# Eight memory recalls as three f32r products each, in an attention and gated-FFN kernel on one Trainium2 core

## The chip, the cores and the metric

The kernel runs on one core of one Trainium2 chip. The metric is the device time of one execution in microseconds (us), lower is better. A time is the median of several runs of the compiled program. Beside it one execution is taken by the hardware profiler; its span reaches from the first to the last instruction of the core.

Five engines work on their own instruction queues: TensorE (PE in the profile, with its weight loads as PEld), VectorE (DVE), ScalarE (ACT), GpSimd (POOL) and SyncE (SP), which issues most DMAs here.

## What is computed

The input x is 2048 tokens of 448 values. After a layer norm it goes through 16-head attention with a compressive memory (four segments of 512 tokens, attended one by one) and, in parallel, through a gated FFN of width 1792. Both results are added to x.

```
xn = layernorm(x)                              # [2048, 448]
q, k, v = xn @ wq, xn @ wk, xn @ wv            # 16 heads of 28, 4 segments of 512 tokens
for each segment s:
    a_dot = softmax(q_s k_s^T * scale + mask) v_s
    a_mem = (phi(q_s) M) / (phi(q_s) z + 1e-6) # phi(t) = t + 1 if t > 0 else exp(t)
    o_s   = g * a_mem + (1 - g) * a_dot        # g = sigmoid(beta), one per head
    M, z  = M + phi(k_s)^T v_s, z + sum(phi(k_s))
out = x + o @ wo + (sigmoid(xn w_gate) * (xn w_up)) @ w_down
```

The step `phi(q_s) M` is called a recall below. The first segment has an empty memory, so there are three segments with recalls, and in each the sixteen heads are done in four groups of four heads: twelve recalls in all.

## The kernel before, in words

The program has a front part (up to about 163 us), in which the projections, the memory and the recalls are made block by block (a block is a segment of 512 tokens, `b` = 0 to 3), and then a long part in which the FFN's matmuls and the attention scores are interleaved by a fixed ratio, and at the end the output projection.

**Precision.** TensorE takes operands of type f32 or f32r. [...] Where a result must be good to f32, the kernel splits each operand into a high part (the value rounded by an ACT copy to f32r) and a low part (the value less its high part, a DVE subtraction) and adds up three f32r products: high by high, low by high, high by low. The projections `pv` and `pp`, the FFN and the output projection all work so; with 448 inputs in four chunks that makes the eleven products of the list `TERMS`. The recalls of before are the exception: each is one matmul of two f32 operands.

**A block of the front part.** The order on PE, ACT and DVE is the order in which the code is written (`manual_schedule`). For block `b`:

1. Four values steps, `t` = 0 to 3: `values(b, t)` makes eleven products into the PSUM tile `pv` (L335), and ACT copies it into `vst` (L339). In blocks 2 and 3 a recall of the block before, `recall(b-1, t-1, ...)`, follows from `t` = 1 on; the fourth one comes after the first chunk of keys and queries.
2. Seven chunks of keys and queries, `k` = 0 to 6: `keys_queries` makes eleven products into `pp` (L355); ACT writes the high part to `qk` (L356) and makes exp of the negative part in `e` (L360, L361); DVE writes the low part (L362) and finishes the feature map phi in `e` (L365). SP stores `qk` in `qd` (L363) and the query features in `fd` (L368).
3. From chunk `k` = 2 on, `key_rows` transposes the key features of chunk `k` - 2 on PE (`pk`, L375; `e` is the operand loaded as weights) and ACT copies them to `kn` (L377). From `k` = 4 on, `update` makes the memory's increment on PE (`pmm`, L383) and DVE adds it (L389, L390).
4. Meanwhile the layer norm of block `b` + 1 is made: `statistics` on DVE (L294 to L296), `root` on ACT with a load of the square root's table (L301), `rstd` and `normalise` on DVE (L308 to L320), and `turn`, which transposes the normalised tokens on PE (`pt`, L95) and splits them into `xs` on ACT (L97) and DVE (L102, L103).

**A recall.** `phi_queries` loads the query features of a head group from `fd` (L394, SP). PE multiplies them by the group's memory `mst` into the PSUM tile `n2` (L401), which alternates between the banks `m` and `pd`. `pk` and `pmm` use the same two banks. DVE transposes the result (L402), divides and weighs it (L132 to L136) and transposes it back (L404); POOL's queue stores it in `od` (L405). In blocks 2 and 3 the recalls concern the blocks 1 and 2; the recalls of block 3 itself come at the end of the front part, between FFN matmuls.

```
        def recall(b, i, phi):
            ...
            n2 = bank("n2", ("m", "pd")[i % 2])
            T.matmul(n2, mst[b % 2][i], phi, start=True, stop=True)
            V.transpose(ts, n2)
            weigh(sb, ts, gate[:, i:i + 1], MEM_EPS)
            V.transpose(tb, ts)
```

`four_k` is a pool of four buffers of 4 KB per partition: in the front part its tenants are the `qk` tiles.

Of the kernel before, what the change touches and what calls it, by code (L numbers as in the profile page):

```python
# [9 lines left out]
F32 = mybir.dt.float32  # L10
F32R = mybir.dt.float32r
AF = mybir.ActivationFunctionType
# [4 lines left out]
P = 128  # L17
# [6 lines left out]
NT = 4  # L24
# [3 lines left out]
NG = H // HG  # L28
GW = HG * DH
# [32 lines left out]
def kernel(  # L62
# [11 lines left out]
    V, A, G, T = nc.vector, nc.scalar, nc.gpsimd, nc.tensor  # L74
# [33 lines left out]
    def x_block(b):  # L108
        return x[b * L:(b + 1) * L, :].rearrange("(t p) d -> p t d", p=P)
# [5 lines left out]
    def bank(name, tag):  # L115
        return ps.tile([P, L], F32, name=name, tag=tag, bufs=banks[tag])
# [10 lines left out]
    def weigh(pool, num, g, add):  # L127

        r = pool.tile([P, 16], F32, name="rc", bufs=2)
        n3 = num.rearrange("p (m c) -> p m c", c=32)  # L130
        if add:
            V.tensor_scalar_add(r, n3[:, :, DH], add)  # L132
            V.reciprocal(r, r)
        else:
            V.reciprocal(r, n3[:, :, DH])
        V.scalar_tensor_tensor(n3[:, :, :DH], n3[:, :, :DH], g, r.unsqueeze(2).to_broadcast([P, 16, DH]),  # L136
                               op0=ALU.mult, op1=ALU.mult)
# [11 lines left out]
    def four_k(dtype, name):  # L149
        return mid.tile([P, 2, L], dtype, name=name, tag="4k", bufs=4)  # L150
# [125 lines left out]
    with tc.tile_pool(name="front", bufs=2) as sb, tc.manual_schedule(engines=FRONT):  # L276
# [4 lines left out]
        wv = [late_pair("wv") for _ in range(4)]  # L281
        wv = [wv[c // 2][:, c % 2, :] for c in range(8)]
        wqk = [sb.tile([P, 8, P], F32R, name=f"wqk{c}", bufs=1) for c in range(7)]
        mst = [[sb.tile([GW, P], F32, name=f"mst{n}_{i}", bufs=1) for i in range(NG)] for n in range(2)]
        one = sb.tile([P, 1], F32, name="one", bufs=1)
        kn = eight_k(F32, "kn").rearrange("p (t a) n -> p t (a n)", t=NT)

        def statistics(b, t0, steps):

            stats = sb.tile([P, steps, 6], F32, name=f"stats{steps}")  # L290
            mv = sb.tile([P, steps, 2], F32, name=f"mv{steps}")
            vh = sb.tile([P, steps], F32, name=f"vh{steps}")
            for t in range(steps):
                V.bn_stats(stats[:, t, :], acc[b][:, t0 + t, :])  # L294
                V.bn_aggr(mv[:, t, :], stats[:, t, :])
            V.tensor_scalar(vh, mv[:, :, 1], EPS, -0.5, op0=ALU.add, op1=ALU.mult)  # L296
            return mv, vh
# [94 lines left out]
        def phi_queries(b, i):  # L392
            phi = sb.tile([GW, L], F32, name="phi", tag="e", bufs=5)
            nc.sync.dma_start(phi, fd[b][i * GW:(i + 1) * GW])  # L394
            return phi

        def recall(b, i, phi):
            ts = sb.tile([P, L], F32, name="ts", bufs=1)
            tb = sb.tile([P, L], F32, name="tb", bufs=2)
            n2 = bank("n2", ("m", "pd")[i % 2])  # L400
            T.matmul(n2, mst[b % 2][i], phi, start=True, stop=True)  # L401
            V.transpose(ts, n2)  # L402
            weigh(sb, ts, gate[:, i:i + 1], MEM_EPS)
            V.transpose(tb, ts)  # L404
            nc.gpsimd.dma_start(od[b][P * i:P * (i + 1)], tb)  # L405
# [98 lines left out]
        for b in range(NB):  # L504
            last = b == NB - 1
            phi, xn = {}, {}
            if b > 1:
                phi = {i: phi_queries(b - 1, i) for i in range(NG)}
            st = None
            for t in range(3 if b == 0 else 0, NT):  # L510
                values(b, t)
                if b > 1 and t > 0:
                    recall(b - 1, t - 1, phi[t - 1])
                if b == 0:
                    split_qk(t)
                if last:
                    continue
                if t == (3 if b == 0 else 0):
                    mv, vh = statistics(b + 1, 0, NT)
                if t == (3 if b == 0 else 0):  # L520
                    st = mv, vh, root(vh)
                if t == (3 if b == 0 else 2):
                    A.activation(one, ident[:, 0:1], AF.Exp)
            if st and b > 0:
                st = rstd(*st)
                for n in range(2):
                    xn[n] = normalise(b + 1, n, *st[n])
            e = {}
            for k, c in enumerate((3, 4, 5, 6, 0, 1, 2) if last else range(7)):
                e[c] = keys_queries(b, c)  # L530
                if b == 0 and c + 4 < 7:
                    split_qk(c + 4)
                if k == 0:
                    if b > 1:
                        recall(b - 1, NG - 1, phi[NG - 1])
                    if b == 0:
                        st = rstd(*st)
                    if b == 0:
                        A.activation(gate, gate, AF.Exp, scale=-1.0)
                        V.tensor_scalar_add(gate, gate, 1.0)  # L540
                        V.reciprocal(gate, gate)
                        V.tensor_scalar(gate_n, gate, -1.0, 1.0, op0=ALU.mult, op1=ALU.add)
                if (b, k) in ((0, 3), (1, 0)):
                    with tc.issue_after(stored[b, c]):
                        nc.sync.dma_start(acc[b + 2], x_block(b + 2))
                if (b, k) in ((2, 1), (3, 0)):
                    with tc.issue_after(stored[b, c]):
                        next(ffn)
                if last:
                    if k > 0:  # L550
                        next(ffn)
                    if 2 <= k < 6:
                        phi[k - 2] = phi_queries(b, k - 2)
                    if k > 4:
                        begin[k - 5]()
                        recall(b, k - 5, phi[k - 5])
                    continue
                if 2 <= k < 6:
                    key_rows(k - 2, e[k - 2])
                if 4 <= k:  # L560
                    update(b, k - 4)
                if k == 6:
                    update(b, 3)
                n = k - 1 if b == 0 else k + 1
                if 2 <= n < 6:
                    turn(b + 1, n - 2, xn[n - 2])
                if 0 <= n < 4 and n not in xn:
                    xn[n] = normalise(b + 1, n, *st[n])
                if b == 2 and k == 6:
                    next(ffn)  # L570
            if last:
                for i in range(2):
                    for _ in range(FILLS[i]):
                        next(ffn)
                    if i == 0:
                        begin[2]()
                    recall(b, i + 2, phi[i + 2])
# [3 lines left out]
    sb = ctx.enter_context(tc.tile_pool(name="att", bufs=1, reuse_waits="tile"))  # L581
# [203 lines left out]
    with tc.manual_schedule(engines=MANUAL):  # L785
        next(steps)
        k = sum(FILLS) + 6
# [46 lines left out]
```

## Time and profile before

| | |
|---|---|
| median of 3 runs | 687.41 us (687.2 to 687.65) |
| the profiled execution, its own time | 687.43 us |
| its span | 685.7 us |
| PE busy | 679.6 us of the span |
| DVE / ACT / POOL busy | 566.7 / 341.6 / 147.6 us |
| the recall matmuls (L401), busy | 12.3 us, 24 records for 12 recalls |
| block 2 of the front part on PE | 77.88 to 114.82 us |
| block 3 of the front part on PE, up to the first attention scores | 114.82 to 163.18 us |

How to read it: a row of the timeline gives the start and the length of a merged run of equal instructions, the engine, the line of the kernel, the tiles (out<-in) and the count. Matmuls are pipelined, so lengths overlap; what one run of matmuls costs PE is the distance from its start to the start of the next run. Square brackets tell how long the engine sat idle before and who ended it. `SPq` rows are DMA issues on SyncE's queue.

### The profile page before, as it was taken

What the parts mean: (1) busy time and instruction counts of PE and PEld (TensorE: products, weight loads), DVE (VectorE), ACT (ScalarE), POOL (GpSimd) and SP (SyncE); (2) the same over time, 40 slices, a digit from 0 to 9 for tenths busy, and PEclk for the clock granted to TensorE, in tenths of its full rate; (3) what the DMA queues carried; (4) which work ended last, traced back from release to release, by engine and by line L of the source; (5) the groups of instructions that cost most, each with busy time, mean ns of one, the idle gap of its engine ahead of it and who ended that gap; (6) DMA issues with size and microseconds to landing.
All of it is one profiled execution on the core that took longest, in us unless ns stands there. A gap on an engine that the chain in (4) does not pass through costs nothing.

```text
span 685.7 us, 10450 instructions
## 1 busy us (share of the span) xinstructions
PE 679.6 (99%) x3594; PEld 565.5 (82%) x3594; DVE 566.7 (83%) x994; ACT 341.6 (50%) x563; POOL 147.6 (22%) x349
## 2 busy tenths in 40 slices
PE   8999999999999999999999999999999999999997
PEld 7898878778878787887878778787887878778897
DVE  6765695767789998988998889988998899889863
ACT  4837555343554455544556446455643465446220
POOL 3500010101223232222232222232321323212000
PEclk9999999999999999999999999999999999999999
DMA  7446556697242333243324243324342423423342
GB/s 268 179 153 233 204 207 244 246 337 179 71 95 78 94 87 86 58 127 83 85 58 112 58 127 70 99 57 117 82 102 69 97 56 86 95 78 91 93 155 107
DMA packets 45796, 84.37 MB, mean 123 GB/s; under 512 B 6320, under 2 KB 20400, under 8 KB 45232
## 3 DMA queue, kind: packets, MB, share of 16 engines
q1 hardware_dynamic: 42736, 76.37, 36.4%
q0 software_dynamic: 3008, 7.34, 5.2%
q8 instruction: 28, 0.46, 0.3%
q14 instruction: 24, 0.20, 0.1%
HBM read 51.05 MB, written 32.64 MB: 122 GB/s over the span
## 4 chain that ended last, share of the span: by engine, by line
PE 97%; DMA 1%; DVE 1%; SPq 0%; issue 0%; ACT 0%; ACTq 0%
PE pgu L247 41%; PE pd L173 20%; PE pp L355 10%; PE st L612 6%; PE pa L687 5%; PE po L771 5%; PE pv L335 5%; PE pmm L383 2%; PE n L401 2%; DMA acc<-in_x 1%; PE pt L95 1%; PE pk L375 1%; DMA vv<-vd 0%; DVE stats L294 0%; DVE acc L775 0%
## 5 line engine op out<-in xcount | busy, mean ns | idle before, releaser
L247 PE MATMUL pgu<-xs,wgu 128*128 128x512 f32 x1232 | 303.6, 393 | 0.0
L247 PEld LDWEIGHTS pgu<-xs,wgu 128*128 128x128 f32 x1232 | 228.2, 188 | 46.9 <-issue 2.4
L173 PE MATMUL pd<-wdn,hh 128*128 128x448 f32 x672 | 155.9, 367 | 0.0
L173 PEld LDWEIGHTS pd<-wdn,hh 128*128 128x128 f32 x672 | 122.4, 188 | 12.0 <-issue 0.8
L627 POOL TENSOR_SCALAR_AFFINE_SELECT w<-w 128x256 f32<-128x256 f32 (+1 forms) x160 | 80.3, 505 | 240.9 <-ACT w L616 192.4
L667 ACT ACTIVATE w<-w 128x1024 f32<-128x1024 f32 (+1 forms) x96 | 87.4, 916 | 88.4 <-DVE w L666 87.9
L666 DVE TENSOR_TENSOR w<-w,mb 128x1024 f32<-128x1024 f32 (+1 forms) x96 | 98.6, 1035 | 0.2
L616 ACT ACTIVATE w<-st 128x512 f32<-128x512 f32 x128 | 74.7, 591 | 43.2 <-PE st L612 42.9
L629 DVE TRANSPOSE_TENSOR_REDUCE mx<-w 128x32 f32<-128x1024 f32 x64 | 78.8, 1231 | 14.8 <-POOL w L627 14.7
L355 PE MATMUL pp<-xs,wqk 128*128 128x512 f32 x308 | 77.7, 401 | 0.0
L174 DVE TENSOR_TENSOR acc<-pd,acc 128x448 f32<-128x448 f32 x112 | 67.2, 600 | 1.1 <-PE pd L173 1.1
L355 PEld LDWEIGHTS pp<-xs,wqk 128*128 128x128 f32 x308 | 56.8, 188 | 13.4 <-issue 2.4
L612 PE MATMUL st<-qk 84*128 84x128 f32 (+3 forms) x256 | 62.3, 313 | 0.1
L258 ACT ACTIVATE hh<-sg 128x512 fp32r<-128x512 f32 x56 | 35.2, 628 | 53.4 <-DVE sg L256 42.2
L612 PEld LDWEIGHTS st<-qk 84*128 84x128 f32 x256 | 47.7, 189 | 7.5 <-ACT w L616 0.7
L255 ACT ACTIVATE sg<-pgu 128x512 f32<-128x512 f32 x56 | 33.1, 592 | 36.2 <-PE pgu L247 36.2
L656 DVE STREAM_TRANSPOSE mb<-top 128x1024 f32<-128x1024 f32 x32 | 39.7, 1242 | 12.6 <-POOL top L653 12.3
L362 DVE TENSOR_TENSOR qk<-pp,qk 128x512 fp32r<-128x512 f32 x28 | 19.3, 689 | 29.8 <-ACT e L360 23.7
L259 DVE SCALAR_TENSOR_TENSOR hh<-sg,hh 128x512 fp32r<-128x512 f32 x56 | 38.9, 694 | 2.8 <-ACT hh L258 2.4
L335 PE MATMUL pv<-wv,xs 128*128 128x448 f32 x176 | 39.6, 376 | 0.4 <-DVE xs L102 0.3
L256 DVE SCALAR_TENSOR_TENSOR sg<-sg,pgu 128x512 f32<-128x512 f32 x56 | 37.3, 667 | 1.7 <-PE pgu L247 1.5
L687 PE MATMUL pa<-w,vv 128*32 128x128 f32 (+3 forms) x512 | 37.9, 436 | 0.0
(100 smaller groups left out, 639.5 us busy)
## 6 DMA issues: line engine op xcount, KB each, us to landing
qk<-qd SPq DMA_DIRECT2D x192, 112.0 KB
qd<-qk SPq DMA_DIRECT2D x28, 512.0 KB
raw<-in_w_ffn SPq DMA_DIRECT2D x14, 512.0 KB
vd<-vst SPq DMA_DIRECT2D x4, 1024.0 KB
vv<-vd SPq DMA_DIRECT2D x16, 256.0 KB
od<-w POOLq DMA_DIRECT2D x16, 256.0 KB, 3.9
sums<-od SPq DMA_DIRECT2D x32, 128.0 KB
out<-acc SPq DMA_DIRECT2D x16, 224.0 KB
```

The lines of the kernel that those rows point to most:

```text
L173: T.matmul(pd[:, :D], l, r, start=n == 0, stop=n == len(mms) - 1)
L174: V.tensor_add(acc[b][:, t, :], pd[:, :D], acc[b][:, t, :])
L247: T.matmul(dst, wgu[f][:, w, side * P:(side + 1) * P], xs[b][:, a, :], start=n == 0, stop=n == len(TERMS) - 1)
L335: T.matmul(pv[:, :D], xs[b][:, a, t * P:(t + 1) * P], wv[w], start=n == 0, stop=n == len(TERMS) - 1)
L355: T.matmul(pp, wqk[c][:, w, :], xs[b][:, a, :], start=n == 0, stop=n == len(TERMS) - 1)
L612: T.matmul(st[:, at:at + L - kb * P], self.qk[:KS, 1, h, kb * P:(kb + 1) * P], self.qk[:KS, 0, h, kb * P:], start=True, stop=True)
L616: A.activation(w, st, AF.Copy)
L627: G.affine_select(d, d, pattern=pattern, base=0, channel_multiplier=-1, compare_op=ALU.is_ge, fill=MASK)
L629: V.tensor_reduce(mx[:, 16 * (n - 1):16 * (n + 1)], w3[:, n // 2, :2 * L].rearrange("p (b n) -> p b n", n=32), axis=mybir.AxisListType.X, ...
L666: V.tensor_sub(w, w, m)
L667: A.activation(w, w, AF.Exp, scale=SCALE)
L687: T.matmul(pa[32 * j:32 * j + 32, kb * P:], self.vv[:, kb, 32 * j:32 * j + 32], self.pairs[j // 2].block(j % 2, kb), start=kb == 0, stop=k ...
```

## The change

The eight recalls of blocks 1 and 2 (those made during blocks 2 and 3) become three f32r products each. The four recalls of block 3 stay f32 matmuls.

- `memory_parts` splits the memory of all four head groups at once, at the start of a block: an ACT copy and a DVE subtraction of 112x512, into the tile `ms`. For that the four memory tiles of a parity become one tile.
- `parts` splits the features of one head group, 112x512 again, into `phis`. Group 0 is split at the start of the block, group `t` + 1 after `values(b, t)`, so a group is split two values steps before its recall.
- `ms` and the four `phis` tiles take buffers of the pool `four_k`.
- `statistics` now stands ahead of the recall of its step (it was behind it; in step 0 there is none). `root` comes one step later in block 2 (`t` = 1), and `turn` one chunk later there (chunks 2 to 5, they were 1 to 4), with the normalisation of tokens 2 and 3.

```diff
--- before.py
+++ after.py
@@ -281,7 +281,8 @@
         wv = [late_pair("wv") for _ in range(4)]
         wv = [wv[c // 2][:, c % 2, :] for c in range(8)]
         wqk = [sb.tile([P, 8, P], F32R, name=f"wqk{c}", bufs=1) for c in range(7)]
-        mst = [[sb.tile([GW, P], F32, name=f"mst{n}_{i}", bufs=1) for i in range(NG)] for n in range(2)]
+        memory = [sb.tile([GW, NG, P], F32, name=f"mst{n}", bufs=1) for n in range(2)]
+        mst = [[m[:, i, :] for i in range(NG)] for m in memory]
         one = sb.tile([P, 1], F32, name="one", bufs=1)
         kn = eight_k(F32, "kn").rearrange("p (t a) n -> p t (a n)", t=NT)
 
@@ -394,11 +395,27 @@
             nc.sync.dma_start(phi, fd[b][i * GW:(i + 1) * GW])
             return phi
 
+        def memory_parts(b):
+
+            m = four_k(F32R, "ms")[:GW].rearrange("p a (i n) -> p a i n", i=NG)
+            A.activation(m[:, 0], memory[b % 2], AF.Copy)
+            V.tensor_sub(m[:, 1], memory[b % 2], m[:, 0].bitcast(F32))
+            return m
+
+        def parts(i, phi, m):
+
+            f = four_k(F32R, "phis")[:GW]
+            A.activation(f[:, 0, :], phi, AF.Copy)
+            V.tensor_sub(f[:, 1, :], phi, f[:, 0, :].bitcast(F32))
+            return [(m[:, a, i, :], f[:, w, :]) for a, w in ((0, 0), (1, 0), (0, 1))]
+
         def recall(b, i, phi):
             ts = sb.tile([P, L], F32, name="ts", bufs=1)
             tb = sb.tile([P, L], F32, name="tb", bufs=2)
             n2 = bank("n2", ("m", "pd")[i % 2])
-            T.matmul(n2, mst[b % 2][i], phi, start=True, stop=True)
+            terms = phi if isinstance(phi, list) else [(mst[b % 2][i], phi)]
+            for n, (l, r) in enumerate(terms):
+                T.matmul(n2, l, r, start=n == 0, stop=n == len(terms) - 1)
             V.transpose(ts, n2)
             weigh(sb, ts, gate[:, i:i + 1], MEM_EPS)
             V.transpose(tb, ts)
@@ -506,18 +523,23 @@
             phi, xn = {}, {}
             if b > 1:
                 phi = {i: phi_queries(b - 1, i) for i in range(NG)}
+                mp = memory_parts(b - 1)
+                phi[0] = parts(0, phi[0], mp)
             st = None
             for t in range(3 if b == 0 else 0, NT):
                 values(b, t)
-                if b > 1 and t > 0:
-                    recall(b - 1, t - 1, phi[t - 1])
+                if not last and t == (3 if b == 0 else 0):
+                    mv, vh = statistics(b + 1, 0, NT)
+                if b > 1:
+                    if t < NG - 1:
+                        phi[t + 1] = parts(t + 1, phi[t + 1], mp)
+                    if t > 0:
+                        recall(b - 1, t - 1, phi[t - 1])
                 if b == 0:
                     split_qk(t)
                 if last:
                     continue
-                if t == (3 if b == 0 else 0):
-                    mv, vh = statistics(b + 1, 0, NT)
-                if t == (3 if b == 0 else 0):
+                if t == (3, 0, 1)[b]:
                     st = mv, vh, root(vh)
                 if t == (3 if b == 0 else 2):
                     A.activation(one, ident[:, 0:1], AF.Exp)
@@ -561,7 +583,7 @@
                     update(b, k - 4)
                 if k == 6:
                     update(b, 3)
-                n = k - 1 if b == 0 else k + 1
+                n = k + (-1, 1, 0, 0)[b]
                 if 2 <= n < 6:
                     turn(b + 1, n - 2, xn[n - 2])
                 if 0 <= n < 4 and n not in xn:
```

How the order moves at three places follows.

PE in block 2, from the last values step to the third key chunk. `xs_67` are block 2's tokens; `n_...` are the recalls' results. Before:

```order
L335 MATMUL pv<-wv,xs_67 128x448 x11
L401 MATMUL n_1003<-phi,mst_2_128 128x512
L355 MATMUL pp<-xs_67,wqk_115 128x512 x11
L401 MATMUL n_1045<-phi,mst_3_129 128x512
L355 MATMUL pp<-xs_67,wqk_116 128x512 x11
L95 MATMUL pt<-ident,xn 128x128 x4
L355 MATMUL pp<-xs_67,wqk_117 128x512 x11
L375 MATMUL pk<-ident,e 128x128 x4
```

With the change:

```order
L336 MATMUL pv<-wv,xs_67 128x448 x11
L418 MATMUL n_1016<-phis,ms 128x512 x3
L356 MATMUL pp<-xs_67,wqk_115 128x512 x11
L418 MATMUL n_1060<-phis,ms 128x512 x3
L356 MATMUL pp<-xs_67,wqk_116 128x512 x11
L356 MATMUL pp<-xs_67,wqk_117 128x512 x11
L376 MATMUL pk<-ident,e 128x128 x4
```

Each recall is three matmuls, and no token transposition (`pt`) stands between the second and the third chunk any more; the first transposition of key rows (`pk`) follows the third chunk directly.

DVE at the start of block 2, from the end of the statistics to the second recall's result. The subtractions for the memory (L402, `ms`) and for group 0 (L409, `phis`) stand ahead of the statistics and are not shown. Before:

```order
L294 BN_STATS stats_924<-acc_72 128x6
L295 BN_AGGR mv_925<-stats_924 128x2
L296 TENSOR_SCALAR vh_926<-mv_925 128x4
L402 STREAM_TRANSPOSE ts<-n_953 128x512
L132 TENSOR_SCALAR rc<-ts 128x16
L133 RECIPROCAL rc<-rc 128x16
L136 SCALAR_TENSOR_TENSOR ts<-ts,gate,rc 128x16x28
L404 STREAM_TRANSPOSE tb<-ts 128x512
L402 STREAM_TRANSPOSE ts<-n_977 128x512
```

With the change:

```order
L295 BN_STATS stats_924<-acc_72 128x6
L296 BN_AGGR mv_925<-stats_924 128x2
L297 TENSOR_SCALAR vh_926<-mv_925 128x4
L409 TENSOR_TENSOR phis<-phi,phis 112x512 x2
L419 STREAM_TRANSPOSE ts<-n_957 128x512
L132 TENSOR_SCALAR rc<-ts 128x16
L133 RECIPROCAL rc<-rc 128x16
L136 SCALAR_TENSOR_TENSOR ts<-ts,gate,rc 128x16x28
L421 STREAM_TRANSPOSE tb<-ts 128x512
L409 TENSOR_TENSOR phis<-phi,phis 112x512
L419 STREAM_TRANSPOSE ts<-n_988 128x512
```

The subtractions of groups 1 and 2 now stand ahead of the first recall's result, that of group 3 behind it.

SP at the end of block 2, the loads of the features that block 3's recalls need. Before:

```order
L368 DMA fd_85<-e 128x512
L394 DMA phi<-fd_85 112x512
L363 DMA qd_81<-qk 128x1024
L368 DMA fd_85<-e 128x512
L394 DMA phi<-fd_85 112x512 x3
```

With the change:

```order
L369 DMA fd_85<-e 128x512
L395 DMA phi<-fd_85 112x512 x2
L364 DMA qd_81<-qk 128x1024
L369 DMA fd_85<-e 128x512
L395 DMA phi<-fd_85 112x512 x2
```

The load of group 1's features has moved ahead of the last chunk's two stores.

## The prediction, made before the changed kernel was run

> **What bounds the kernel now.** I read the page first: how busy the engines are, and which engine the chain of work that ended last ran through. Then the list of PE's waits.
>
> ```profile
> span 685.7 us, 10450 instructions
> PE 679.6 (99%) x3594; PEld 565.5 (82%) x3594; DVE 566.7 (83%) x994; ACT 341.6 (50%) x563; POOL 147.6 (22%) x349
> PE 97%; DMA 1%; DVE 1%; SPq 0%; issue 0%; ACT 0%; ACTq 0%
> PE warm L442 <- POOL ident masks.py:199: 1.5, 1, 1.5
> PE pt L95 <- DVE xn L320: 0.5, 1, 0.5
> PE pv L335 <- DVE xs L102: 0.3, 1, 0.3
> ```
>
> PE is the bound from end to end. All its recorded waits are 2.3 us, and they lie in the first microseconds, which the change does not touch. So a microsecond of PE time taken away is a microsecond gained, and a microsecond for which PE is made to wait is one lost. The question is how much PE work goes, and whether PE must now wait for something that was early before.
>
> **The price of a recall.** On PE a run costs the distance from its start to the next run's start. These rows of PE's timeline give the price of each kind.
>
> ```profile
> 44.45 9.05 PE L335 MATMUL pv<-wv,xs 128*128 128x448 f32 x44
> 53.34 5.15 PE L355 MATMUL pp<-xs,wqk 128*128 128x512 f32 x22
> 58.33 0.60 PE L95 MATMUL pt<-ident,xn 128*128 128x128 f32 x4
> ...
> 82.38 1.02 PE L401 MATMUL n<-phi,mst 112*128 112x512 f32 x2
> 82.84 2.77 PE L335 MATMUL pv<-wv,xs 128*128 128x448 f32 x11
> 85.45 1.02 PE L401 MATMUL n<-phi,mst 112*128 112x512 f32 x2
> ...
> 91.89 1.02 PE L401 MATMUL n<-phi,mst 112*128 112x512 f32 x2
> 92.35 3.09 PE L355 MATMUL pp<-xs,wqk 128*128 128x512 f32 x11
> 95.27 0.60 PE L95 MATMUL pt<-ident,xn 128*128 128x128 f32 x4
> 95.63 2.77 PE L355 MATMUL pp<-xs,wqk 128*128 128x512 f32 x11
> 98.23 0.60 PE L375 MATMUL pk<-ident,e 128*128 128x128 f32 x4
> ...
> 101.62 0.60 PE L375 MATMUL pk<-ident,e 128*128 128x128 f32 x4
> ```
>
> An f32r product of 448 columns costs (53.34 - 44.45) / 44 = 0.202 us, one of 512 columns (58.33 - 53.34) / 22 = 0.227 us. The recall and eleven `pv` products behind it take 85.45 - 82.38 = 3.07 us; less 11 x 0.202 = 2.22 that leaves 0.85 for the f32 recall. With eleven `pp` products behind it, 95.27 - 91.89 = 3.38, less 2.50, it is 0.88. I take 0.867. Three f32r products of 512 columns cost 3 x 0.227 = 0.680; their weight loads hide behind the product before, as those of `pp` do. Gain 0.187 a recall, **1.50 us for eight**.
>
> [...]
>
> A small second gain: products that follow a transposition start slowly. Eleven `pp` after a `pt` take 98.23 - 95.63 = 2.60 us, not 2.50. In block 2 the `pt` between the second and third chunk goes, and the four groups of `pt` now all stand behind `pk` or `pmm`, where that start is paid anyway: **0.10 us**. Together 1.60 us of PE work goes.
>
> **What comes in on the other engines.** Ten ACT copies and ten DVE subtractions of 112x512 with both inputs in SBUF. The nearest rows are an ACT operation of 512 columns from SBUF, 0.63 us, and the split of down weights with 448 columns on DVE: 0.61 us long, but the next instruction starts 0.53 us later. Scaled to 512 columns I take 0.60 us from start to start and 0.68 us to the result (bounds: 0.53 and 0.68 for the first).
>
> ```profile
> 77.53 0.63 ACT L361 ACTIVATE e<-e 128x512 f32<-128x512 f32 x1
> ...
> 85.65 0.54 ACT L339 ACTIVATE vst<-pv 128x448 f32<-128x448 f32 x1 [1.90 <-PE pv L335]
> ...
> 147.02 0.61 DVE L86 TENSOR_TENSOR wdn<-rawd,wdn 128x448 fp32r<-128x448 f32 x1
> 147.55 0.71 DVE L402 STREAM_TRANSPOSE ts<-n 128x512 f32<-128x512 f32 x1
> ```
>
> [...]
>
> ACT has room: it waited 1.90 us for PE at the copy of 85.65. Behind a split that waits there for its load stands only the copy that empties a `pv` bank, and that bank is needed two steps later. DVE is the engine to follow. Its rows in block 2, with the loads of the features:
>
> ```profile
> 79.86 0.62 DVE L294 BATCH_NORM_STATS2 stats<-acc 128x6 f32<-128x448 f32 x1
> ...
> 82.91 0.17 DVE L296 TENSOR_SCALAR vh<-mv 128x4 f32<-128x4 f32 x1
> ...
> 86.51 0.72 DVE L402 STREAM_TRANSPOSE ts<-n 128x512 f32<-128x512 f32 x1 [0.39 <-PE n L401]
> ...
> 92.18 0.13 DVE L308 RECIPROCAL y<-y 128x4 f32<-128x4 f32 x1
> ...
> 93.86 0.68 DVE L362 TENSOR_TENSOR qk<-pp,qk 128x512 fp32r<-128x512 f32 x1
> 94.47 0.68 DVE L365 SCALAR_TENSOR_TENSOR e<-pp,e 128x512 f32<-128x512 f32 x1
> 95.06 0.70 DVE L402 STREAM_TRANSPOSE ts<-n 128x512 f32<-128x512 f32 x1
> ...
> 97.65 0.65 DVE L362 TENSOR_TENSOR qk<-pp,qk 128x512 fp32r<-128x512 f32 x1
> 98.23 0.68 DVE L365 SCALAR_TENSOR_TENSOR e<-pp,e 128x512 f32<-128x512 f32 x1
> ```
>
> ```profile
> 78.91 0.32 SPq L368 DMA_DIRECT2D fd<-e  x1
> ...
> 81.82 0.32 SPq L394 DMA_DIRECT2D phi<-fd  x1
> ...
> SPq L394 <- DMA fd<-e: 1.9, 1, 1.9
> ```
>
> In a values step DVE waited 0.39 us for PE's recall. Now PE's step is 0.19 us shorter and DVE's 0.60 us longer, so DVE falls behind. The walk, on the old clock, nothing ahead of 79.86 being changed: memory split 79.86, group 0 80.46, statistics 81.06 (3.05 us to `vh`), group 1 about 84.3, free at 84.9. Group 2's features are the load issued at 81.82, which waited for the store of 78.91 to land, 2.9 us after issue. A load of a little less size I give 2.65 us (bounds 2.3 and 2.9): landed 84.47, copied by ACT 85.10, on DVE from 85.15 to 85.75. Then without a pause: a recall's five operations take 97.65 - 95.06 = 2.59 us; first recall to 88.34, group 3 to 88.94, second to 91.53, third to 94.12; root's rest and two normalisations (93.86 - 92.18 = 1.68) to 95.80; low part of chunk 0 and its `e`, whose result is there at 97.09; the fourth recall from 97.00 to 99.59; chunk 1, with `e` at 100.85.
>
> PE in the meantime: second recall at 82.38 + 0.68 + 2.22 = 85.28 (its last product needs group 1's low part, there at 85.0), third at 88.18, fourth at 91.36, chunks 1 and 2 from 92.04 to 97.03. A recall's bank, `m` or `pd`, is emptied by the first of DVE's five operations for the recall two before, at 85.75 + 0.72 = 86.5 and 88.94 + 0.72 = 89.7: in time. Then come the key rows. They load `e` as weights, which PE would do 0.23 us ahead of the product, at 96.80. `e` of chunk 0 is there at 97.09, with 0.05 for the signal: 0.34 us late. The next key rows are wanted one chunk later, at 100.53 counted with that delay (`pk`, `pt` and a chunk take 101.62 - 98.23 = 3.39 us); `e` of chunk 1 comes at 100.90: another 0.37 us. Before, `e` of chunk 0 was ready 3 us ahead of its `pk` at 98.23. From then on DVE gains: a chunk costs it about 2.6 us, PE 3.4 and more. **Loss in block 2: 0.71 us**, with bounds: the load 0.35 earlier or 0.25 later, the subtraction's pace 0.14 less or 0.16 more in the two that count, and 0.23 less if the late weights cost no reload: 0 to 1.1.
>
> In block 3 nothing of the kind follows. DVE stood idle for 2.37 us ahead of the first recall:
>
> ```profile
> 112.02 0.32 SPq L368 DMA_DIRECT2D fd<-e  x1
> ...
> 118.97 0.31 SPq L394 DMA_DIRECT2D phi<-fd  x1
> ...
> 119.32 1.02 PE L401 MATMUL n<-phi,mst 112*128 112x512 f32 x2
> ...
> 120.38 0.72 DVE L402 STREAM_TRANSPOSE ts<-n 128x512 f32<-128x512 f32 x1 [2.37 <-PE n L401]
> ```
>
> That covers memory and groups 0 and 1. Group 2, loaded at 118.97, is on the chip at 121.62, split by ACT and DVE at about 122.9, and the first recall's transpose stands behind it on DVE, until 123.65. PE wants that bank for the third recall at 119.32 + 2 x 2.90 = 125.1: **1.45 us to spare, no loss**. No key rows are made there.
>
> **Sum.** 1.50 + 0.10 - 0.71 = 0.89 us less PE time. The profiled execution had 685.7 us of span and 687.43 in all, 1.73 around it: 684.8 + 1.73 = 686.54. The median of the runs is 687.41, so 686.5 there. What can be told from no change here is 0.2%, 1.37 us, so this counts as no change.
>
> **Rivals.**
>
> The full gain. DVE's lag stays below PE's need: 687.41 - 1.60 = 685.8, faster. It needs the low ends of the bounds above together; for it, each of the two late arrivals is short (0.34 and 0.37 us); against it, the steps' sum, in which DVE has 0.25 us of idling left.
>
> The gain is eaten. The lag is 1 us more than I count, by slower DVE operations or a later load: the loss is 1.7 us, time 687.5. Nothing in the rows speaks for it beyond the tightness of the walk.
>
> SP's queue in block 3, slower. Group 1's load now stands ahead of the last two stores on SP and waits for the store of 112.02. If that lands late, both stores, the loads of groups 2 and 3, DVE and the banks follow. It decides once group 2 lands over 1.45 us late; to be slower by 0.2% it must give back 0.89 and cost 1.37, so 3.7 us late: 688.8 or more. Against it: at the 2.9 us of the other store it lands at 114.9, as early as the last chunk's store is wanted.
>
> **How the numbers follow.** The forecast 0.60 (its own range 686.2 to 687.1), the full gain 0.19, the gain eaten 0.12, slower 0.09. Faster by over 0.2% is the full gain, 0.19; within 0.2% the first and third, 0.72; slower 0.09. The range runs from the full gain, 685.8, past the eaten gain to 688.2, short of the slow case.
>
> **What would show it.** In the profile after: recall records x3 with 0.68 us from start to start; about 0.7 us of PE waiting for DVE's `e` at the first two `pk` of block 2 and none in block 3; DVE without a pause from 85.2 to 100. No wait there: the full gain. A wait at recalls 3 or 4 of block 3: the queue. Recalls of other than 0.68 us make the first term wrong.

## The result: slower by half a per cent

| | before | after |
|---|---|---|
| median | 687.5 us (687.2 to 687.69, 6 runs) | 691.09 us (690.0 to 692.28, 6 runs) |
| the profiled execution, its own time | 687.43 us | 690.49 us |
| its span | 685.7 us | 688.8 us |

The ratio after to before is 1.0054, with the interval 1.0044 to 1.0065. The forecast was 686.5 us, with a range up to 688.2, so the time lies outside it on the slow side. The profiled execution of after is one of its quicker ones; it shows 3.1 of the 3.6 us that the medians differ by.

The page of the changed kernel (span; busy time, share and count of each engine; the chain that ended last, by engine), and then the list of PE's waits (total us, times, longest):

```profile
span 688.8 us, 10483 instructions
PE 679.7 (99%) x3602; PEld 566.6 (82%) x3602; DVE 572.5 (83%) x1004; ACT 346.6 (50%) x573; POOL 147.3 (21%) x349
PE 85%; DVE 6%; DMA 6%; issue 1%; ACT 1%; SPq 0%; ACTq 0%; DVEq 0%
...
PE st L634 <- ACT w L638: 1.5, 1, 1.5
...
PE st L634 <- DMA qk<-qd: 0.7, 1, 0.7
PE pk L376 <- DVE e L366: 0.4, 2, 0.3
PE pd L173 <- DVE ts L419: 0.4, 1, 0.4
```

Before, PE carried 97% of the chain and had no wait behind the first microseconds. Now it carries 85%, and DVE and DMA carry 6% each. The wait of `pk` for `e` is in the prediction; the other three, at the scores `st` and the FFN's `pd`, lie behind block 3's chunks, of which the prediction does not speak.

**Up to 145 us the forecast holds.** PE's timeline of after (start, length, engine, line, tiles, count, and the idle time before it with its releaser):

```profile
82.25 0.87 PE L418 MATMUL n<-phis,ms 112*128 112x512 f32 x3
85.17 0.87 PE L418 MATMUL n<-phis,ms 112*128 112x512 f32 x3
...
92.02 5.15 PE L356 MATMUL pp<-xs,wqk 128*128 128x512 f32 x22
97.45 0.66 PE L376 MATMUL pk<-ident,e 128*128 128x128 f32 x4 [0.28 <-DVE e L366]
...
101.22 0.66 PE L376 MATMUL pk<-ident,e 128*128 128x128 f32 x4 [0.16 <-DVE e L366]
...
114.90 0.45 PE L336 MATMUL pv<-wv,xs 128*128 128x448 f32 x1
```

A recall has three records, and a recall with eleven `pv` takes 85.17 - 82.25 = 2.92 us; it took 3.07. The gain is 0.15 us a recall (forecast 0.187). The first `pk` starts at 97.45 (forecast 97.37): 22 `pp` at 0.227 us end at 97.01, so 0.44 us are lost there. From one `pk` to the next it takes 101.22 - 97.45 = 3.77 instead of 3.39, another 0.38. Block 2 loses 0.82 us (forecast 0.71) and gains four times 0.15. The brackets show only 0.28 + 0.16 of the loss as idle time; the rest is the loading of `e` as weights, which now starts with the product (both at 97.45) and before started 0.23 us ahead of it (98.00 against 98.23). From its first recall to the start of block 3 it takes 114.90 - 82.25 = 32.65 us, and before 114.82 - 82.38 = 32.44: 0.21 more. Block 3 then gains: its last FFN matmuls ahead of the next recall start at 145.04, and before at 145.58, so after is 0.54 us ahead there.

**From 145 us on the time goes.** PE at the first scores of after, and then a row of before:

```profile
163.82 0.47 PE L634 MATMUL st<-qk 84*128 84x512 f32 x1 [0.68 <-DMA qk<-qd]
...
167.38 1.47 PE L173 MATMUL pd<-wdn,hh 128*128 128x448 f32 x6 [0.36 <-DVE ts L419]
...
170.34 0.50 PE L634 MATMUL st<-qk 84*128 84x512 f32 x1 [1.49 <-ACT w L638]
```

```profile
167.42 0.40 PE L612 MATMUL st<-qk 84*128 84x512 f32 x1
```

Before, the first `st` stood at 163.18, the first `pd` at 166.16 and the `st` behind it at 167.42. The lag of after against before is 0.64 us at the first, 1.22 at the second and 2.92 at the third, where PE waits 1.49 us for ACT, which copies the scores `st` into `w`. At the end of the span it is 3.1 us.

**Followed back.** The chain of waits of after, between 125 and 175 us (start, length, what):

```profile
137.17 6.16 DMA fd<-e
...
151.37 7.44 DMA raw<-in_w_ffn
158.90 1.07 ACT wgu L85
```

Read from below: a weight copy on ACT waited for a load of 7.44 us, and further up a load of query features (`phi`) waited 6.16 us for a store of features (`fd`) to land. What ties them together is SP's queue: in after, none of its rows here passes one that waits ahead of it. The fourth chunk's `qk`, for instance, was finished by DVE at 139.78 + 0.69 = 140.47, but its store, which stands behind the `phi` load that waited until 143.34, left at 144.23. The rows, first of after, then of before:

```profile
132.82 0.34 SPq L364 DMA_DIRECT2D qd<-qk  x1
...
143.34 0.32 SPq L395 DMA_DIRECT2D phi<-fd  x1
...
149.11 0.32 SPq L395 DMA_DIRECT2D phi<-fd  x1
...
151.37 0.49 SPq L184 DMA_DIRECT2D raw<-in_w_ffn  x1
```

```profile
130.87 0.34 SPq L363 DMA_DIRECT2D qd<-qk  x1
...
139.45 0.75 SPq L394 DMA_DIRECT2D phi<-fd  x1
...
145.61 0.32 SPq L394 DMA_DIRECT2D phi<-fd  x1
...
148.80 0.49 SPq L184 DMA_DIRECT2D raw<-in_w_ffn  x1
```

The first store of block 3 leaves 1.95 us later, and the next but one behind it is the first of two FFN weight loads that the code ties to this store (`issue_after`; called the first loads of the FFN below). The first `phi` load, which waits for the stores of `fd` to land, leaves 3.89 us later, the third 3.50, and the weight load of 151.37 behind it 2.57. The table by stretch (us, busy time of PE, PEld, DVE, ACT, POOL with counts, PE's clock, DMA share, GB/s), before and then after, shows what the DMA engines did around those two microseconds:

```profile
131.00:137.00 6.00, 6.00 (x29) 4.95 (x28) 4.20 (x9) 2.88 (x6) 0.54 (x1) 1.00 0.93 327
```

```profile
131.00:137.00 6.00, 6.00 (x28) 4.99 (x27) 5.83 (x11) 3.42 (x6) 1.08 (x2) 1.00 0.66 217
```

The 16 DMA engines were 0.93 busy and are 0.66 busy: 0.27 x 6 = 1.6 us of all of them unused, while DVE is busy for 5.83 of the 6 us. What was not moved then has to be moved later, and there is little room: before, the engines are 0.93 busy from 131 to 143 us, 0.92 to 155 and 1.00 to 165. DVE itself has caught up by the fourth chunk (its low part starts at 139.78, before at 140.33). ACT's copy of the weights loaded at 151.37, the last weight copy ahead of the first scores, shows the end of it, before and then after, with the copy that stands ahead of it in after and DVE's row behind it:

```profile
154.05 1.06 ACT L85 ACTIVATE wgu<-raw 128x1024 fp32r<-128x1024 f32 x1 [0.46 <-DMA raw<-in_w_ffn]
```

```profile
157.09 0.58 ACT L85 ACTIVATE wdn<-rawd 128x448 fp32r<-128x448 f32 x1 [4.18 <-DMA rawd<-in_w_ffn]
158.90 1.06 ACT L85 ACTIVATE wgu<-raw 128x1024 fp32r<-128x1024 f32 x1 [1.23 <-DMA raw<-in_w_ffn]
```

```profile
159.99 1.22 DVE L86 TENSOR_TENSOR wgu<-raw,wgu 128x1024 fp32r<-128x1024 f32 x1 [5.16 <-ACT wgu L85]
```

The copy starts 4.85 us later; ACT waited 4.18 us for the load of the copy ahead of it, then 1.23 for this one. DVE, which makes the weights' low part next, is idle for 5.16 us there, and what stands behind on DVE and ACT comes late to PE's `st` and `pd`.

**Where DVE became late.** PE's first recall in block 3 of after, ACT's copy of group 2's features and DVE's rows, and then DVE's of before:

```profile
119.40 0.87 PE L418 MATMUL n<-phis,ms 112*128 112x512 f32 x3
```

```profile
122.31 0.63 ACT L408 ACTIVATE phis<-phi 112x512 fp32r<-112x512 f32 x1 [2.17 <-DMA phi<-fd]
```

```profile
122.97 0.69 DVE L409 TENSOR_TENSOR phis<-phi,phis 112x512 fp32r<-112x512 f32 x1 [3.07 <-ACT phis L408]
123.58 0.71 DVE L419 STREAM_TRANSPOSE ts<-n 128x512 f32<-128x512 f32 x1
...
126.18 0.65 DVE L409 TENSOR_TENSOR phis<-phi,phis 112x512 fp32r<-112x512 f32 x1
126.75 0.71 DVE L419 STREAM_TRANSPOSE ts<-n 128x512 f32<-128x512 f32 x1
...
132.14 0.65 DVE L363 TENSOR_TENSOR qk<-pp,qk 128x512 fp32r<-128x512 f32 x1
```

```profile
123.45 0.72 DVE L402 STREAM_TRANSPOSE ts<-n 128x512 f32<-128x512 f32 x1 [0.39 <-PE n L401]
...
126.52 0.72 DVE L402 STREAM_TRANSPOSE ts<-n 128x512 f32<-128x512 f32 x1 [0.38 <-PE n L401]
...
130.15 0.69 DVE L362 TENSOR_TENSOR qk<-pp,qk 128x512 fp32r<-128x512 f32 x1 [0.95 <-ACT e L360]
```

The low part of group 2 (122.97) stands ahead of the first recall's result on DVE and waits 3.07 us for ACT, which waits for the load. The recall's product is ready meanwhile: its three matmuls start at 119.40 and, at 0.70 us, are over by about 120.3. DVE takes nothing from behind the waiting split in these 3.07 us. So the first result starts at 123.58, 3.20 us later than the 120.38 of before. Group 3's low part adds 126.75 - 126.18 = 0.57. The idle times of before, 0.39, 0.38 and 0.95, are all there was to make it up: 3.20 + 0.57 - 1.72 = 2.05 us late at chunk 0's low part; the rows say 132.14 - 130.15 = 1.99.

### The profile page after: what moved, and what is told of

It is laid out like the page before. It is cut to its first block, busy times and chain, and to the rows that moved or that the text cites. A ratio compares the mean times of both kernels' runs of the same rounds, so it can differ in the third digit from the quotient of the medians.

```text
span 688.8 us, 10483 instructions
## 1 busy us (share of the span) xinstructions
PE 679.7 (99%) x3602; PEld 566.6 (82%) x3602; DVE 572.5 (83%) x1004; ACT 346.6 (50%) x573; POOL 147.3 (21%) x349
## 4 chain that ended last, share of the span: by engine, by line
PE 85%; DVE 6%; DMA 6%; issue 1%; ACT 1%; SPq 0%; ACTq 0%; DVEq 0%
PE pgu L247 38%; PE pd L173 20%; PE pp L356 7%; PE st L634 6%; PE pa L709 5%; PE po L793 5%; PE pv L336 2%; DMA fd<-e 2%; DMA phi<-fd 1%; DMA raw<-in_w_ffn 1%; PE pmm L384 1%; DMA acc<-in_x 1%; DVE ts L419 1%; DVE ts L136 1%; PE pt L95 1%
## 5 line engine op out<-in xcount | busy, mean ns | idle before, releaser
L356 PE MATMUL pp<-xs,wqk 128*128 128x512 f32 x308 | 75.8, 396 | 0.0
L336 PE MATMUL pv<-wv,xs 128*128 128x448 f32 x176 | 38.2, 367 | 0.2
```

Source lines behind the costliest of these rows:

```text
L336: T.matmul(pv[:, :D], xs[b][:, a, t * P:(t + 1) * P], wv[w], start=n == 0, stop=n == len(TERMS) - 1)
L356: T.matmul(pp, wqk[c][:, w, :], xs[b][:, a, :], start=n == 0, stop=n == len(TERMS) - 1)
```

## The experiments

**Theory A**, from these rows: block 3 loses because the split that waits on DVE, ahead of work that is ready, makes the stores late, and through SP's queue and the DMA engines the weight loads behind them. The rivals are that the products, the splits or DVE's sum of work cost the time by themselves, wherever the split stands; each expectation names its own. Every time is the median; the ratio is to runs of the kernel before on the same chip.

**1 and 2. The products in one block only.** The recalls of the other block stay f32 matmuls. The diff is the first run's; the second has 3 in place of 2.

```diff
-                mp = memory_parts(b - 1)
-                phi[0] = parts(0, phi[0], mp)
+                if b == 2:
+                    mp = memory_parts(b - 1)
+                    phi[0] = parts(0, phi[0], mp)
...
-                    if t < NG - 1:
+                    if b == 2 and t < NG - 1:
```

In the second run, `root` and `turn` of block 2 also stand where they stood before.

> Three products for the recalls made in block 2 alone; block 3's four recalls are f32 matmuls again. Theory A (in block 3 DVE's added work makes the first key and query chunk's stores late, the FFN's first weight loads wait behind them on SP, and a DMA that is full from 130 to 165 us passes the lateness on to the first attention scores): block 3 runs as before, block 2 costs what its trace shows, 0.08 us (114.90 against 114.82), so 687.5 us, and no PE wait at the first scores. Theory B (the loss comes from what block 2 does, e.g. its later transpositions): 691. Theory C (each block with splits costs half): 689.3.

Measured: 687.5 us (687.29 to 687.66), ratio 1.0003, interval 0.9993 to 1.0012. The first store left at 130.84, as before, and behind the first microseconds PE waits only at `pk` for `e`, twice.

> Three products for the recalls made in block 3 alone; block 2 has f32 recalls, root and transpositions as before. Theory A: the whole loss is here, 690.5 to 691.5 us, with PE waiting at the first scores. Theory B: 686.8, the gain of four recalls without a loss. Theory C: 689.3.

Measured: 690.42 us (689.55 to 691.69), ratio 1.0047, 1.0032 to 1.0062. The store left at 132.21, the last weight copy on ACT started at 159.95. The loss is block 3's alone, and it does not need the changes that block 2 sees. Block 2's own sum, 0.82 lost less 0.60 gained, is the 0.2 us that the first run is over the kernel before. The profile of the second run is of the slowest of its four executions (691.69).

**3. The same work on DVE in block 3, in another order.** The split of group `t` + 1 stands behind the step's recall, in block 3 alone.

```diff
-                    if t < NG - 1:
+                    if t < NG - 1 and b < 3:
                         phi[t + 1] = parts(t + 1, phi[t + 1], mp)
                     if t > 0:
                         recall(b - 1, t - 1, phi[t - 1])
+                    if t < NG - 1 and b == 3:
+                        phi[t + 1] = parts(t + 1, phi[t + 1], mp)
```

> As the change, but in block 3 the split of group t+1 stands behind the recall of its step and not ahead of it, so that DVE need not wait for group 2's features before it takes the first recall's result. The same instructions otherwise. Theory A: DVE starts the first recall's result at about 120.2 us instead of 123.6, the first chunk's store goes out at 131 instead of 132.8, the FFN loads at 132.2 instead of 133.9: 687.0 us (0.5 gained up to there stays), at most 687.8. If the splits' work itself, the pool of four buffers or the three products cause the loss: 690 to 691.

Measured: 686.93 us (686.78 to 690.49, nine of ten at or below 687.14), ratio 1.0001, 0.999 to 1.0012. DVE's first recall result in block 3, first store and last weight copy of this kernel:

```profile
120.32 0.72 DVE L419 STREAM_TRANSPOSE ts<-n 128x512 f32<-128x512 f32 x1 [0.40 <-PE n L418]
```

```profile
130.53 0.34 SPq L364 DMA_DIRECT2D qd<-qk  x1
```

```profile
154.61 1.06 ACT L85 ACTIVATE wgu<-raw 128x1024 fp32r<-128x1024 f32 x1 [1.55 <-DMA raw<-in_w_ffn]
```

Nothing was taken out, and the 4 us are gone: DVE takes the first result 3.26 us earlier than in after (123.58). So neither the products nor the splits nor the buffers of `four_k` that they take cost them; the place of the wait does. What slowed the tenth execution, at 690.49, is not known.

**4 and 5. The kernel before, made late.** Multiplications that nobody reads (112x128) are put on DVE ahead of block 3's first chunk, nine in the diff and sixteen in the second run; the recalls stay f32.

```diff
+            if last:
+                for _ in range(9):
+                    dm = sb.tile([GW, P], F32, name="dm")
+                    V.tensor_mul(dm, heads[:GW], heads[:GW])
```

> The kernel before, with nine added DVE multiplications of 112x128 whose result is not used, in block 3 ahead of the first chunk's work on DVE: about 2 us of DVE time; f32 recalls, no splits. No PE instruction waits for them directly. Theory A: the first chunk's stores and the FFN loads go out up to 2 us late, and the time grows to 689 to 691 us. If DVE's lateness there is harmless: 687.5.

Measured: 687.32 us, ratio 1.0001, 0.9992 to 1.0011: a miss. DVE's idle 0.95 us took up half of the added 1.8 us; the store left at 131.48, only 0.61 us late, and this costs nothing.

> As the run with nine added multiplications, but with sixteen. Nine moved the first chunk's store only from 130.87 to 131.48 us, since DVE had been idle there; sixteen should bring it to about 132.9, where the changed kernel has it (132.82), with none of the change's splits or products. Theory A with a threshold (lateness of the stores up to some 1 us is absorbed, beyond that the loads of block 3's features and of the FFN's weights fall into each other): 689.5 to 691 us, with PE waiting at the first scores. If lateness of these stores is not the cause: 687.3 to 687.5.

Measured: 689.53 us (688.94 to 690.05), ratio 1.0033, 1.0021 to 1.0045. The store left at 132.99, 2.12 us late. The same stretch, and ACT's last weight copy:

```profile
131.00:137.00 6.00, 6.00 (x28) 4.95 (x28) 5.86 (x16) 2.92 (x6) 0.54 (x1) 1.00 0.56 175
```

```profile
158.11 1.06 ACT L85 ACTIVATE wgu<-raw 128x1024 fp32r<-128x1024 f32 x1 [1.79 <-DMA raw<-in_w_ffn]
```

Without one f32r recall in the kernel, lateness on DVE at this place alone makes it slower, through the same rows. The delay here costs 2.3 us, that of the change some 4.

**6. The stores late, but the FFN's first loads not behind them.** In after, the first loads of the FFN are recorded in block 3's second values step, no longer to be issued behind the first store.

```diff
+                if last and t == 1:
+                    next(ffn)
...
-                if (b, k) in ((2, 1), (3, 0)):
+                if (b, k) == (2, 1):
                     with tc.issue_after(stored[b, c]):
                         next(ffn)
```

> As the change, with the FFN's first loads not tied behind the store of block 3's first chunk: they are issued during block 2, where the DMA engines are half idle. DVE's lateness stays. Theory A, with the queued weights (0.7 MB, about 2 us of a full DMA) as the main weight in the backlog: 686.5 to 687.8 us. If the late stores and feature loads alone are enough: 689 to 691.

Measured: 686.86 us (686.58 to 687.46), ratio 0.9996, 0.9986 to 1.0005. In the trace the weight loads `raw` that leave at 133.93 and 143.71 in after leave at 108.21 and 118.31, so the edit also brings forward the load behind the two that were tied. The store left at 132.62, as late as in after; the DMA engines were even emptier from 131 to 137 us, 0.50 busy; but the last weight copy on ACT started at 154.65, and PE waited for nothing at the scores. So a late store alone cost nothing here: the loss needed the weight loads behind it in the stretch from 131 to 165 us, where the DMA engines of before are 0.92 to 1.00 busy.

**7. The low parts on GpSimd.** In after, all ten subtractions move from DVE to GpSimd.

```diff
-            V.tensor_sub(m[:, 1], memory[b % 2], m[:, 0].bitcast(F32))
+            G.tensor_sub(m[:, 1], memory[b % 2], m[:, 0].bitcast(F32))
...
-            V.tensor_sub(f[:, 1, :], phi, f[:, 0, :].bitcast(F32))
+            G.tensor_sub(f[:, 1, :], phi, f[:, 0, :].bitcast(F32))
```

> As the change, with the ten subtractions for the low parts on GpSimd and not on DVE. GpSimd's 128x512 subtractions of the weights took 1.3 us each in the profile after, and it is nearly idle in blocks 2 and 3; each low part should be there at least 0.4 us ahead of its product. DVE then does what it did before: no lateness of the stores, no PE wait at the key rows; PE keeps the whole 1.6 us: 685.7 to 686.1 us. If the three products or the ACT copies cause the loss: 689 or more. If DVE is held up by GpSimd's reads: between.

Measured: 691.27 us (689.76 to 692.53), ratio 1.0061, 1.0048 to 1.0073: a miss by 5 us. The store left at 132.62 all the same. DVE's rows and one of GpSimd's show DVE held up:

```profile
78.98 1.09 DVE L391 TENSOR_TENSOR mst<-mst,dm 112x128 f32<-112x128 f32 x1
...
88.60 1.59 DVE L132 TENSOR_SCALAR rc<-ts 128x16 f32<-128x16 f32 x1
...
124.97 2.50 DVE L132 TENSOR_SCALAR rc<-ts 128x16 f32<-128x16 f32 x1
```

```profile
78.63 1.30 POOL L402 TENSOR_TENSOR ms<-mst,ms 112x512 fp32r<-112x512 f32 x1 [12.74 <-ACT ms L401]
```

While GpSimd subtracts, the `mst` addition takes 1.09 us (0.29 otherwise) and ends at 80.07, 0.14 us after GpSimd's row; the small `rc` operation takes 1.59 and 2.50 us (0.18 otherwise). The `mst` row has two inputs, `rc` has one. Not every DVE operation is held up: the reciprocal (L133), which starts at 85.38, inside GpSimd's subtraction of 85.22 to 86.52, takes its usual 0.25 us. What decides which ones wait is not shown by any run here. In block 3 PE's first recall also waits 0.51 us for GpSimd's low part, so this run does not separate the cost of that wait from the cost of DVE's delay.

**8 and 9. Block 2: the statistics taken out of the way.** The order of run 3, and the statistics for block 3 (3.05 us of DVE) are made in block 1, where DVE was idle. In the second, the FFN's first loads leave early as in run 6.

```diff
-                if not last and t == (3 if b == 0 else 0):
+                if b < 2 and t == (3 if b == 0 else 0):
                     mv, vh = statistics(b + 1, 0, NT)
+                if b == 2 and t == 0:
+                    mv, vh = third
...
+                if b == 1 and k in (4, 5):
+                    if k == 4:
+                        third = statistics(3, 0, 2, NT)
+                    else:
+                        third = statistics(3, 2, 2, NT, third)
```

> As the run with block 3's splits behind the recall's result, and block 3's statistics are made in block 1 (two tiles behind chunk 4, two behind chunk 5, where VectorE stood 1.63 and 1.96 us idle) and no longer behind block 2's first value product (3.05 us of VectorE). The first split of block 2, its recalls and its first `e` then come up to 3 us earlier. Theory A (what block 2 lost, 0.7 to 0.8 us, is VectorE late with `e` at the first two `pk`, and block 3 loses nothing once the stores are on time): no wait `pk` <- DVE `e`, and 686.0 to 686.4, a ratio of 0.998 to 0.999. Rival B (the wait at `pk` is ScalarE's or the recalls', not the statistics'): the wait stays and the time is that of the split behind, 686.9. Rival C (the statistics hold up block 1's low parts by 1.2 us each, and PE waits there for the bank instead): 687.0 to 687.6.

Measured: 686.98 us (686.64 to 690.05), ratio 1.0, 0.9991 to 1.0009. Theory A's figure was missed; `pk` still waited, and rival B's figure came out. DVE's rows in block 2 of this kernel:

```profile
85.35 0.69 DVE L415 TENSOR_TENSOR phis<-phi,phis 112x512 fp32r<-112x512 f32 x1 [1.34 <-ACT phis L414]
85.96 0.71 DVE L425 STREAM_TRANSPOSE ts<-n 128x512 f32<-128x512 f32 x1
```

The 3 us that were freed became idling ahead of the splits. Group 2's low part stood ahead of the first recall's result here too, and the result started at 85.96, when it had started at 85.88 in run 3. The prediction's walk of block 2 has the same wait in it, at 85.15.

> As the last, and the first loads of the FFN are no longer tied behind block 3's first store, so that they leave before it. Theory A: with the stores on time nothing waits for these loads any more, 686.0 to 686.4, the same as the last within 0.2. Rival D (the DMA engines' full stretch to 165 us costs something by itself, and whatever is drawn ahead of it gains): 685.4 to 685.9.

Measured: 686.93 us (686.75 to 687.39), ratio 0.9995, 0.9986 to 1.0004: the same as run 8 within 0.2 us, as expected, but theory A's figure (686.0 to 686.4) was missed again; rival D's gain did not come. With the stores on time the early loads are worth nothing.

**10 and 11. The split behind the recall in both blocks**, with the statistics in block 1 (run 10) and with them left in block 2 (run 11). Against after, run 11 is:

```diff
-                    if t < NG - 1:
+                    if t == 0:
                         phi[t + 1] = parts(t + 1, phi[t + 1], mp)
                     if t > 0:
                         recall(b - 1, t - 1, phi[t - 1])
+                    if 0 < t < NG - 1:
+                        phi[t + 1] = parts(t + 1, phi[t + 1], mp)
```

> As the run with the splits behind in block 3 and the statistics in block 1, and now block 2's split of group t+1 stands behind the step's recall result as well. In that run VectorE had the statistics' 3 us free and stood idle 2.17 and 1.34 us for ScalarE's copies of the feature rows, ahead of the first recall result at 85.96. Theory A (the split's wait, ahead of work that is ready, is what makes block 2's first two `e` late, as it made block 3's stores late): the first recall result starts at 83.9 to 84.1, the first two `pk` wait for no `e`, PE's gap in front of them falls from 0.61 and 0.55 us to 0.23 each, and the time is 686.1 to 686.4, a ratio near 0.9985. Rival B (VectorE's work between is too much whatever stands in front): the gaps stay and the time is 686.9.

Measured: 686.11 us (685.9 to 687.88), ratio 0.9986, 0.9977 to 0.9995; the first recall result starts at 83.83, within 0.1 of the expectation.

> The change with the split of group t+1 behind the step's recall result in blocks 2 and 3, and nothing else: the statistics stay in block 2. VectorE is done with them at 84.1 and splits group 1, so the first recall result starts at 84.7 (85.9 with the split behind in block 3 alone), 1.2 us earlier, where 0.3 us were missing at the first `pk`. Theory A: no wait at `pk`, 686.1 to 686.4, as the last. Rival B: 686.9. Rival E (the statistics matter after all): the wait halves, 686.6.

Measured: 686.04 us (685.92 to 687.27), ratio 0.9984, 0.9975 to 0.9994; span 684.5. Both did what theory A says, and differ by 0.07 us, which tells nothing between them. DVE and then PE in run 11:

```profile
84.83 0.71 DVE L419 STREAM_TRANSPOSE ts<-n 128x512 f32<-128x512 f32 x1
```

```profile
92.15 5.15 PE L356 MATMUL pp<-xs,wqk 128*128 128x512 f32 x22
97.14 0.60 PE L376 MATMUL pk<-ident,e 128*128 128x128 f32 x4
...
100.55 0.64 PE L376 MATMUL pk<-ident,e 128*128 128x128 f32 x4
```

The first recall's result starts 1.05 us earlier than in run 3. The 22 `pp` are followed by `pk` at once (97.14 - 92.15 = 4.99), the next `pk` comes 3.41 us later, and no wait for `e` is left. This version beats both kernels: 1.2 us below before, while after is 3.6 above it, by the order of two statements.

**The runs side by side.** The start of the store, and the start of ACT's last weight copy (the `wgu<-raw` of 128x1024):

| kernel | first store, us | last weight copy, us | against before, us |
|---|---|---|---|
| before | 130.87 | 154.05 | 0 |
| 1, block 2 only | 130.84 | 154.38 | +0.2 |
| 3, split behind in block 3 | 130.53 | 154.61 | -0.4 |
| 11, split behind in both | 129.85 | 153.01 | -1.2 |
| 4, before delayed, nine | 131.48 | 154.47 | 0.0 |
| 6, loads early | 132.62 | 154.65 | -0.4 |
| 5, before delayed, sixteen | 132.99 | 158.11 | +2.3 |
| after | 132.82 | 158.90 | +3.6 |
| 2, block 3 only | 132.21 | 159.95 | +3.1 |
| 7, low parts on GpSimd | 132.62 | 161.00 | +4.1 |

The starts are those of one profiled execution each; for runs 2 and 7 it was the slowest (691.69 and 692.53). The intervals of runs 3 and 6 include no change. Where the copy started by 154.65, nothing was lost; where it started at 158.11 or later, 2 to 4 us were. The store's start does not decide alone: at 132.62 run 6 loses nothing and run 7 some 4 us, and run 2 loses more at 132.21 than run 5 at 132.99.

## Why the prediction was wrong

**What bounds the kernel.** PE does, before and in run 11, with 97% of the chain in both; this held.

**The gain, 1.60 us.** Right in kind, too large. Three products cost 2.92 - 2.22 = 0.70 us, not 0.680, and the f32 recall with eleven `pv` behind it 0.85, not the mean 0.867: 8 x 0.15 = 1.2 us. Where PE waits for nothing behind the first microseconds, in run 11, the span falls by 685.7 - 684.5 = 1.2 us and the median by 1.20. The 0.10 us for the `pt` group isn't to be seen apart in that sum.

**The loss in block 2, 0.71 us.** Right: 0.82 by the rows, at the two `pk` and for the reason given. Run 11 takes it away. What the prediction did not see is that it needn't be: it walked DVE in the order written and took the wait for group 2's features as given, when the recall's product lay ready behind it.

**The failing step: "In block 3 nothing of the kind follows", "1.45 us to spare, no loss. No key rows are made there."** The walk had the wait in it (group 2 split at about 122.9, the first result behind it) and then asked a single question of it, whether PE gets its bank back in time. It does; PE doesn't wait at a recall in block 3's values steps. But DVE's next works are chunk 0's low part and `e`, and behind them stand SP's stores, and behind the first of these, by `issue_after`, the FFN's first weight loads. Rows of before and the walk's own figures would have told it: the walk has the first result done at 123.65, before at 120.38 + 0.72 = 121.10, so 2.55 us late; with 0.60 for group 3's split that is 3.15, and DVE's three idle times between 123 and 131 us sum to 1.72: 1.4 us late at chunk 0. The runs showed 1.99 there, a store 1.95 us late and, with the weight loads behind it, some 4 us lost. The prediction followed DVE's lateness in block 3 to PE's bank alone.

**The rival that came nearest** was SP's queue in block 3. It looked for the damage in group 1's load ahead of two stores, with 1.45 us as the point from which it decides. ACT's copy of group 2 started at 122.31 against a forecast landing of 121.62, so the load was within the 1.45 us and this rival's condition was not met. The queue and the sign were its own, the place was another: the stores of block 3's chunks, ten microseconds later. Its chance of 0.09 was too low also because the forecast's chain ended at PE's bank.

**What stays open.** That lateness on DVE at chunk 0, with the weight loads behind the store, makes the kernel slower is shown by runs 2 to 6. The size is not derived: 2.12 us of delay put into the kernel before cost 2.3 us, the change's 1.95 us of it some 4 (3.6 in the median, plus the 0.4 that runs 3 and 6 gain: 0.6 from block 3's recalls less block 2's 0.2). Stores, `phi` loads and weight loads all leave between 132.82 and 151.37 us in after, and which transfer displaced which was not tried one by one. Single executions of runs 3 and 8 at 690.49 and 690.05, with medians of 686.93 and 686.98, are not explained; no profile shows them.

## What to carry to other kernels

Put an operation that waits for a load behind the work that is already ready, not ahead of it: DVE idled for 3.07 us with a result ready behind the wait from about 120.3 us on, and here the order of two statements was worth 4.8 us (3.6 + 1.2, each against before), and the saved work itself 1.2. When a change makes an engine late, follow every consumer to its end, the stores and what is queued behind them on SP included, and set the lateness against the engine's idle times in the profile of before.

## What was not expected of the hardware

- The cost of a late store did not grow in proportion. In the kernel before, with 0.61 us of delay nothing was lost and the DMA engines fell to 0.81 busy from 131 to 137 us; with 2.12 us they fell to 0.56 and the last weight load ahead of the scores, issued 2.14 us later (150.94 against 148.80), was used 4.06 us later (158.11 against 154.05).
- The two kernels that lose most scatter more: after ranges over 2.3 us in six runs, run 7 over 2.8 in five, and the kernel before over 0.5 in six. Runs 3 and 8 range over 3.7 and 3.4 us, but through one execution each; their others lie within 0.4 and 1.1 us.
- While GpSimd subtracted, not only DVE's two-input `mst` addition took longer (1.09 us, 0.29 otherwise) but also the one-input `rc` of 128x16: 1.59 and 2.50 us, 0.18 otherwise.
